# Cluster attention and two MLPs on one core: the softmax reciprocals and scalings of two units taken together

## The chip, the core and the metric

The kernel runs on one core of a Trainium2 chip. The metric is device time in microseconds (us) of one execution. The kernel before was timed three times: the median is 837.77 us, the lowest 836.97, the highest 840.25. The profile that is read below comes from another execution, which took 837.66 us.

## The reference

What is computed, in numpy: attention in which a query sees only the keys of its own cluster, followed by two MLPs. Shapes: q, k and v are (2, 8, 768, 64), there are 16 centroids a head; x is (1536, 512), the first MLP is 1536 wide inside and the second 2048.

```python
q_assign = np.argmax(np.einsum('bhsd,hcd->bhsc', q_n, c_n), axis=-1)   # q_n, k_n, c_n: rows of unit length
k_assign = np.argmax(np.einsum('bhsd,hcd->bhsc', k_n, c_n), axis=-1)
mask = q_assign[:, :, :, None] == k_assign[:, :, None, :]
scores = scale * np.matmul(q, k.transpose(0, 1, 3, 2))
scores = np.where(mask, scores, -1000000000.0)
scores = scores - np.max(scores, axis=-1, keepdims=True)
attn = np.exp(scores)
attn = attn / (np.sum(attn, axis=-1, keepdims=True) + 1e-09)
attn_out = np.matmul(attn, v)
x = attn_out.transpose(0, 2, 1, 3).reshape(B * S, H * D)
x = (1.0 / (1.0 + np.exp(-(x @ w_gate))) * (x @ w_val)) @ w_out
h = np.maximum(x @ w_in2, 0.0)
out = h * h @ w_out2
```

## The kernel before, in words

The kernel has an attention stage and then the two MLPs. The order of the instructions on each engine is the order in which the code issues them; each engine works through its own queue in that order, and semaphores hold an instruction until what it needs is there.

The attention is cut into 96 **units** of 128 queries: 8 pairs of heads (`pairs`), two heads each (`e`), two halves of the queries (`n`), three blocks of 128 in each half (`j`). The main loop (line 888) has one **step** n for each unit and a few more at the end. A unit passes through several steps:

- Its scores, 128 queries by 768 keys in four matmuls into PSUM tile `s`, are issued by TensorE in the step before its own (`scores`, line 776).
- In step n VectorE takes the negative maximum of each row (line 897), and ScalarE the exponential into tile `p`, with the row sums as a second result (line 918; the trace shows the fetch of the sums as a short instruction of its own, ACTIVATION_READ_ACCUMULATOR). GpSimd adds 1e-9 to the sums (line 932).
- In step n+1 VectorE takes the reciprocal of the sums and GpSimd scales `p` by it, in place (`normalise`, lines 847 and 848).
- In step n+3 (`LAG = 3`) the scaled unit is moved out (`evac`): TensorE transposes its six blocks into two PSUM tiles `t` (line 794), ScalarE copies them rounded into `pt_hi` (line 796), and VectorE subtracts what was kept to get `pt_lo` (line 802).
- After three units, TensorE multiplies `pt_hi` and `pt_lo` with the values in thirds, one third a step (lines 812 and 813).

The small numbers of a unit lie in tile `nm`, a column each: negative maximum, sum, sum plus 1e-9, reciprocal. There are four buffers for `p` (`LAG + 1`), three PSUM tiles for `t`, two for `s`.

Within a step the engines get their work in this order. TensorE: the transposes of the unit of three steps before, the scores of the next unit, one third of an attention product, and preparation of the next pair of heads. VectorE: the maximum, what was left over of the preparation (`drain`), the reciprocal, the two subtractions of line 802, preparation. ScalarE: the two copies of line 796, the exponential. GpSimd: the scaling of the unit before, the addition of 1e-9, and then what `late`, `todo` and `decoding` hold for this step: splitting the values (lines 754 and 757), adding up and splitting a finished output for the MLP (lines 832, 841 and 843), a part of the argmax (line 661), in some steps a part of the decoding of the first MLP weights (lines 224 and 227). These go by tables of step numbers (`STEPS`, `VALUES`, `SUMS`, `EARLY_PARTS`).

After the 96 units the MLPs follow; their matmuls (lines 339 to 341 and 417) and the decoding of their weights don't touch the lines of the change.

Of the kernel before, what the change touches and what calls it, by code (L numbers as in the profile page):

```python
# [8 lines left out]
F32 = mybir.dt.float32  # L9
# [5 lines left out]
ALU = mybir.AluOpType  # L15
AX = mybir.AxisListType
# [52 lines left out]
def cluster_attention_two_mlps(  # L69
# [13 lines left out]
    nc = tc.nc  # L83
    B, H, S, D = q.shape
    NCL = centroids.shape[1]
    P = 128
# [6 lines left out]
    NH = HB * P  # L93
# [47 lines left out]
    def open_weights():  # L141
        for nm, bufs in (("wraw", 2), ("wtmp", 1), ("w", NW - EARLY)):
            pools[nm] = ctx.enter_context(tc.tile_pool(name=nm, bufs=bufs, side="right", reuse_waits="tile"))
        for _ in range(2):
            fetch()


    def early(spare):
        body, mag, top = (spare[:, t * DM : (t + 1) * DM] for t in range(3))
        raw = spare[:, 4 * DM :].rearrange("p (f t) -> p f t", t=2)  # L150
        fetch(raw)
        ring.extend(w_early)
        return [part for n in range(EARLY) for part in early_parts(n, (w_early[n], body, mag, f32(top)), raw)]
# [155 lines left out]
    with tc.manual_schedule():  # L309
# [4 lines left out]
        ones = const.tile([P, 1], F32, name="ones")  # L314
# [129 lines left out]
        with ExitStack() as ac:  # L444
# [8 lines left out]
            sm = ac.enter_context(tc.tile_pool(name="sm", bufs=6))  # L453
# [308 lines left out]
            units = [(i, e, n, j) for i in range(len(pairs)) for e in range(2) for n in range(2) for j in range(HB)]  # L762
            Pt, PThi, PTlo, xs, nms, decoding = {}, {}, {}, {}, {}, {}
            UPP, N = len(units) // len(pairs), len(units)
# [5 lines left out]
            def scores(u):  # L770
                i, e, n, j = u
                c = n * HB + j
                st = ps_s.tile([P, 2, 512], F32, name="s")
                for a in range(2):
                    for m in range(2):
                        nc.tensor.matmul(  # L776
                            st[:, m, :NH],
                            Q[i, e][: DEPTH[e][a], a, c * P : (c + 1) * P],
                            K[i, e][: DEPTH[e][a], a, m * NH : (m + 1) * NH],
                            start=(a == 0),  # L780
                            stop=(a == 1),
                        )
                return st

            def evac(u, a):

                i, e, n, j = u
                if a == 0 and j == 0:
                    PThi[i, e, n] = ptp.tile([P, NB, NH], F32R, name="pt_hi")
                    PTlo[i, e, n] = ptp.tile([P, NB, NH], F32R, name="pt_lo")  # L790
                tp = ps_t.tile([P, HB, P], F32, name="t")
                for m in range(HB):
                    c = a * HB + m
                    nc.tensor.transpose(tp[:, m, :], Pt[u][:, c * P : (c + 1) * P], ident)  # L794
                hi = PThi[i, e, n][:, a * HB : (a + 1) * HB, j * P : (j + 1) * P]
                nc.scalar.copy(hi, tp)  # L796
                return tp, hi

            def low(u, a, tp, hi):
                i, e, n, j = u  # L800
                lo = PTlo[i, e, n][:, a * HB : (a + 1) * HB, j * P : (j + 1) * P]
                nc.vector.tensor_tensor(out=lo, in0=tp, in1=f32(hi), op=ALU.subtract)  # L802
# [40 lines left out]
                        nc.gpsimd.tensor_tensor(out=lo, in0=src, in1=f32(hi), op=ALU.subtract)  # L843
                    c0 = c1

            def normalise(p, nm):
                nc.vector.reciprocal(out=nm[:, 3:4], in_=nm[:, 2:3])  # L847
                nc.gpsimd.tensor_scalar(out=p, in0=p, scalar1=nm[:, 3:4], scalar2=ones, op0=ALU.mult, op1=ALU.mult)  # L848

            load(0, "kq")  # L850
            load(1, "kq")
# [11 lines left out]
            def drain():  # L863
                while posts:
                    posts.pop(0)()

            def do(f, *args):
                post = f(*args)
                if post is not None:
                    posts.append(post)  # L870
# [7 lines left out]
            outs, late, st = {}, {}, {}  # L878
# [9 lines left out]
            for n in range(N + LAG + 4):  # L888
                u = units[n] if n < N else None
                w = units[n - LAG] if 0 <= n - LAG < N else None  # L890
                if n == N - UPP:
                    drain()
                    pc.close()
                    open_weights()
                if u is not None:
                    nms[n] = sm.tile([P, 4], F32, name="nm")
                    nc.vector.tensor_reduce(out=nms[n][:, 0:1], in_=st[n][:, :, :NH], axis=AX.XY, op=ALU.max, negate=True)  # L897
                nm = nms.pop(n - 1, None)
                if nm is not None:
                    p = Pt[units[n - 1]]  # L900
                drain()
                if nm is not None and w is None:
                    normalise(p, nm)
                if n == N:
                    sc.close()
                    for nm_, bufs in (("sg", 2), ("act", NA)):
                        pools[nm_] = ctx.enter_context(tc.tile_pool(name=nm_, bufs=bufs, side="right", reuse_waits="tile"))
                    pools["a"] = ctx.enter_context(
                        tc.tile_pool(name="ps_a", bufs=4, space=PSUM, side="right", reuse_waits="tile")
                    )  # L910
                if w is not None:
                    t0, h0 = evac(w, 0)
                    t1, h1 = evac(w, 1)
                if n + 1 < N:
                    st[n + 1] = scores(units[n + 1])
                if u is not None:
                    e = pp.tile([P, S], F32, name="p")
                    nc.scalar.activation(  # L918
                        out=e.rearrange("p (m n) -> p m n", m=2),
                        in_=st.pop(n)[:, :, :NH],  # L920
                        func=AF.Exp,
                        bias=nms[n][:, 0:1],
                        accum_out=nms[n][:, 1:2],
                    )
                    Pt[u] = e
                if w is not None:
                    if nm is not None:
                        normalise(p, nm)
                    low(w, 0, t0, h0)
                    low(w, 1, t1, h1)  # L930
                if u is not None:
                    nc.gpsimd.tensor_scalar(out=nms[n][:, 2:3], in0=nms[n][:, 1:2], scalar1=1e-9, scalar2=None, op0=ALU.add)
                if w is not None:
                    Pt.pop(w)
                    if w[3] == HB - 1:
                        end = n == N + LAG - 1
                        for t in range(3):
                            late.setdefault(n + 1 + (0 if end else t), []).append((attend, (*w[:3], t)))
                        if w[1] == 1:
                            for t in range(3):  # L940
                                at = n + SUMS[w[2]][t] if w[0] < len(pairs) - 1 else n + (3 if end else 6)
                                late.setdefault(at, []).append((finish, (w[0], w[2], t)))
                for f, args in late.pop(n, []):
                    do(f, *args)
                for m, group in enumerate(todo.pop(n, [])):
                    if m:
                        drain()
                    for f in group:
                        do(f)
                if n == 0:  # L950
                    for t, part in enumerate(early(spare)):
                        decoding.setdefault(EARLY_PARTS[t], []).append(part)
                for part in decoding.pop(n, []):
                    part()
                if n - N in LATE_DECODES:
                    for t, part in enumerate(decode_next()):
                        if t < 6:
                            part()
                        else:
                            decoding.setdefault(n + 1, []).append(part)  # L960
                for t, at in enumerate(LATE_GATED):
                    if n == N + at:
                        (gated_first, gated_second)[t % 2](steps[t // 2])
# [46 lines left out]
```

## Time and profile before

| | us |
|---|---|
| median of three runs | 837.77 |
| the profiled execution | 837.66 |
| its span in the profile | 835.9 |
| PE (TensorE matmuls) busy in it | 810.9, 97% of the span |
| DVE (VectorE) busy | 626.1, 75% |
| ACT (ScalarE) busy | 443.8, 53% |
| POOL (GpSimd) busy | 213.6, 26% |

The shares are means over two stages that differ. The attention units are worked on from about 24 to 267 us; GpSimd has all its work there and nothing after 300 us. In the slices of this stage VectorE, ScalarE and GpSimd are all at eight or nine tenths, and in the MLPs TensorE alone is. A row of a timeline names the start, the duration, the engine, the line, the operation with its tiles and shape, and how often it was repeated; a bracket at its end says how long the engine sat idle before it and what it waited for.

### The profile page before, as it was taken

Reading aid. Unit: us, or ns where it says so; the run is one execution under the profiler, and the core shown is the slowest. Engines: PE = TensorE matmul, PEld = TensorE weight load, DVE = VectorE, ACT = ScalarE, POOL = GpSimd, SP = SyncE. Lnnn points to the kernel's source line nnn. Section 1 sums busy time; section 2 is a strip of 40 time slices with the busy share of each in tenths; the row PEclk is TensorE's granted clock in tenths of the full one; section 3 lists DMA queues with packets and bytes.
Section 4 is the critical chain, followed back from the end, with each engine's and each line's share of the span. In section 5 each row is a group of like instructions: output and inputs, shape, how many; then the busy total and the mean of one; then the engine's idle time right before and its main releaser. Section 6 shows DMA issues by size and latency. Waiting matters only on the chain.

```text
span 835.9 us, 11628 instructions
## 1 busy us (share of the span) xinstructions
PE 810.9 (97%) x4069; PEld 689.8 (83%) x4069; DVE 626.1 (75%) x1144; ACT 443.8 (53%) x887; POOL 213.6 (26%) x347
## 2 busy tenths in 40 slices
PE   6998999999999999999999999999999999999998
PEld 4887899999998788888888888887878888888886
DVE  5897999999998378656678657888675697788533
ACT  5787888889897233442333123345654633642530
POOL 3667889888885200000000000000000000000000
PEclk8899999999999999999999999999999999999999
DMA  7454653563421122122111212202221222212012
GB/s 171 92 134 114 135 136 85 127 152 77 100 80 35 45 76 87 45 70 76 58 69 51 75 51 76 76 26 76 76 69 59 74 75 76 76 55 72 26 51 100
DMA packets 63274, 67.01 MB, mean 80 GB/s; under 512 B 28624, under 2 KB 54224, under 8 KB 63216
## 3 DMA queue, kind: packets, MB, share of 16 engines
q1 hardware_dynamic: 63216, 66.27, 28.9%
q8 instruction: 32, 0.52, 0.3%
q14 instruction: 26, 0.21, 0.1%
HBM read 45.12 MB, written 3.15 MB: 58 GB/s over the span
## 4 chain that ended last, share of the span: by engine, by line
PE 77%; DVE 12%; ACT 4%; POOL 3%; issue 2%; DMA 1%; SPq 0%; ACTq 0%; DVEq 0%; POOLq 0%
PE bank_b L417 17%; PE bank_a L340 12%; PE bank_a L341 12%; PE bank_a L339 12%; PE bank_a L417 9%; PE s L776 4%; PE t L794 4%; DVE pt_lo L802 3%; DVE nm L897 2%; PE o L812 2%; PE o L813 2%; POOL p L848 2%; PE t L613 1%; PE t L550 1%; DMA oc<-oc 1%
## 5 line engine op out<-in xcount | busy, mean ns | idle before, releaser
L340 PE MATMUL bank_a<-x_lo,w 128*128 128x512 f32 x480 | 189.3, 394 | 0.5 <-POOL x_lo L843 0.5
L341 PE MATMUL bank_a<-x_hi,w 128*128 128x512 f32 x480 | 187.7, 391 | 2.1 <-DVE w L227 2.1
L339 PE MATMUL bank_a<-x_hi,w 128*128 128x512 f32 x480 | 188.0, 392 | 0.0
L341 PEld LDWEIGHTS bank_a<-x_hi,w 128*128 128x128 f32 x480 | 90.1, 188 | 22.6 <-DVE w L227 2.5
L339 PEld LDWEIGHTS bank_a<-x_hi,w 128*128 128x128 f32 x480 | 90.1, 188 | 21.0
L340 PEld LDWEIGHTS bank_a<-x_lo,w 128*128 128x128 f32 x480 | 90.1, 188 | 20.6 <-POOL x_lo L843 1.0
L383 DVE TENSOR_TENSOR slo<-act,shi 128x512 fp32r<-128x512 f32 x84 | 57.5, 688 | 59.0 <-ACT shi L382 54.5
L802 DVE TENSOR_TENSOR pt_lo<-t,pt_hi 128x384 fp32r<-128x384 f32 x192 | 96.8, 545 | 6.0 <-ACT pt_hi L796 6.0
L848 POOL TENSOR_SCALAR p<-p,nm,ones 128x768 f32<-128x768 f32 x96 | 96.2, 1002 | 18.3 <-DVE nm L847 15.8
L918 ACT ACTIVATE p<-s,nm 128x768 f32<-128x768 f32 x96 | 88.1, 918 | 18.0 <-DVE nm L847 9.1
L776 PE MATMUL s<-st_k,st_q 128*128 128x384 f32 (+1 forms) x384 | 93.2, 365 | 0.9 <-ACT st_k L694 0.9
L897 DVE TENSOR_REDUCE nm<-s 128x1 f32<-128x768 f32 x96 | 91.0, 947 | 2.6 <-PE s L776 2.5
L794 PE MATMUL t<-ident,p 128*128 128x128 f32 x576 | 81.7, 276 | 7.7 <-DVE pt_lo L802 6.0
L796 ACT CAST pt_hi<-t 128x384 fp32r<-128x384 f32 x192 | 83.4, 488 | 8.5 <-PE t L794 7.9
L417 PE MATMUL bank_b<-wo,shi 128*128 128x512 f32 x256 | 79.3, 390 | 0.5 <-DVE wo L227 0.5
L794 PEld LDWEIGHTS t<-ident,p 128*128 128x128 f32 x576 | 65.9, 140 | 16.0 <-issue 3.6
L382 ACT CAST shi<-act 128x512 fp32r<-128x512 f32 x84 | 51.2, 615 | 52.1 <-PE bank_b L417 27.1
L221 ACT CAST w<-wtop 128x512 fp32r<-128x512 f32 x38 | 23.7, 623 | 102.9 <-DVE wtop L239 102.9
L365 DVE TENSOR_TENSOR act<-bank_a,sg 128x512 f32<-128x512 f32 x36 | 24.9, 691 | 66.6 <-PE bank_a L341 62.5
L776 PEld LDWEIGHTS s<-st_k,st_q 128*128 128x128 f32 (+1 forms) x384 | 64.2, 194 | 3.2 <-ACT p L918 1.7
L812 PE MATMUL o<-pt_hi,vt 128*128 128x384 f32 x192 | 65.1, 339 | 0.4 <-ACT oc L818 0.4
L813 PE MATMUL o<-pt_lo,vt 128*128 128x384 f32 x192 | 64.7, 337 | 0.0
(132 smaller groups left out, 1381.1 us busy)
## 6 DMA issues: line engine op xcount, KB each, us to landing
wraw<-in_moe_w_out_dram SPq DMA_DIRECT2D x28, 512.0 KB, 3.2
wraw<-in_moe_w_in_dram SPq DMA_DIRECT2D x16, 512.0 KB, 3.8
wraw<-in_moe_w_gate_dram SPq DMA_DIRECT2D x11, 512.0 KB, 3.6
wraw<-in_moe_w_val_dram SPq DMA_DIRECT2D x11, 512.0 KB, 3.5
nat_v<-in_v_dram SPq DMA_DIRECT2D x8, 384.0 KB, 3.3
st_k<-st_k SPq DMA_DIRECT2D x16, 192.0 KB, 4.7
x<-oc SPq DMA_DIRECT2D x32, 96.0 KB, 2.1
out_dram<-part SPq DMA_DIRECT2D x12, 256.0 KB, 2.1
```

The costliest lines, as they stand in the source:

```text
L339: nc.tensor.matmul(bk, w[:, 0, ks], mov_hi[:, kk], start=(kk == 0), stop=False)
L340: nc.tensor.matmul(bk, w[:, 0, ks], mov_lo[:, kk], start=False, stop=False)
L341: nc.tensor.matmul(bk, w[:, 1, ks], mov_hi[:, kk], start=False, stop=(kk == KD - 1))
L417: nc.tensor.matmul(bk, st, mv, start=(first and n == 0), stop=(last and n == 2))
L776: nc.tensor.matmul(st[:, m, :NH], Q[i, e][: DEPTH[e][a], a, c * P : (c + 1) * P], K[i, e][: DEPTH[e][a], a, m * NH : (m + 1) * NH], start= ...
L794: nc.tensor.transpose(tp[:, m, :], Pt[u][:, c * P : (c + 1) * P], ident)
L796: nc.scalar.copy(hi, tp)
L802: nc.vector.tensor_tensor(out=lo, in0=tp, in1=f32(hi), op=ALU.subtract)
L812: nc.tensor.matmul(o, vt, hi[:, c, :], start=(c == 0), stop=False)
L848: nc.gpsimd.tensor_scalar(out=p, in0=p, scalar1=nm[:, 3:4], scalar2=ones, op0=ALU.mult, op1=ALU.mult)
L897: nc.vector.tensor_reduce(out=nms[n][:, 0:1], in_=st[n][:, :, :NH], axis=AX.XY, op=ALU.max, negate=True)
L918: nc.scalar.activation(out=e.rearrange("p (m n) -> p m n", m=2), in_=st.pop(n)[:, :, :NH], func=AF.Exp, bias=nms[n][:, 0:1], accum_out=nms ...
```

## The change

Two units, an even one and the odd one behind it, share one tile `nm`, now four rows of two columns. The exponential and the maximum of each unit write its own column. The addition of 1e-9 is issued once for both, in the step of the odd unit. `normalise` is issued in the next even step only: one reciprocal of both columns, and then the two scalings, one behind the other.

```diff
-            def normalise(p, nm):
-                nc.vector.reciprocal(out=nm[:, 3:4], in_=nm[:, 2:3])
-                nc.gpsimd.tensor_scalar(out=p, in0=p, scalar1=nm[:, 3:4], scalar2=ones, op0=ALU.mult, op1=ALU.mult)
+            def normalise(ps, nm):
+                nc.vector.reciprocal(out=nm[:, 3], in_=nm[:, 2])
+                for x, p in enumerate(ps):
+                    nc.gpsimd.tensor_scalar(
+                        out=p, in0=p, scalar1=nm[:, 3, x : x + 1], scalar2=ones, op0=ALU.mult, op1=ALU.mult
+                    )
...
                 if u is not None:
-                    nms[n] = sm.tile([P, 4], F32, name="nm")
-                    nc.vector.tensor_reduce(out=nms[n][:, 0:1], in_=st[n][:, :, :NH], axis=AX.XY, op=ALU.max, negate=True)
-                nm = nms.pop(n - 1, None)
+
+                    nms[n] = nms[n - 1] if n % 2 else sm.tile([P, 4, 2], F32, name="nm")
+                    nc.vector.tensor_reduce(out=nms[n][:, 0, n % 2, None], in_=st[n][:, :, :NH], axis=AX.XY, op=ALU.max, negate=True)
+                nm = nms[n - 1] if n % 2 == 0 and 0 < n <= N else None
                 if nm is not None:
-                    p = Pt[units[n - 1]]
+                    p = [Pt[units[x]] for x in (n - 2, n - 1)]
...
-                        bias=nms[n][:, 0:1],
-                        accum_out=nms[n][:, 1:2],
+                        bias=nms[n][:, 0, n % 2, None],
+                        accum_out=nms[n][:, 1, n % 2, None],
...
-                if u is not None:
-                    nc.gpsimd.tensor_scalar(out=nms[n][:, 2:3], in0=nms[n][:, 1:2], scalar1=1e-9, scalar2=None, op0=ALU.add)
+                if u is not None and n % 2:
+                    nc.gpsimd.tensor_scalar(out=nms[n][:, 2], in0=nms[n][:, 1], scalar1=1e-9, scalar2=None, op0=ALU.add)
```

The queues change on two engines. First GpSimd's, for units 84 to 87 (the numbers behind `nm` and `p` tell buffers; lines 932 and 848 of before are lines 936 and 849 now). Before: the scaling of unit 84, and so on to the scaling of unit 87.

```order
L848 TENSOR_SCALAR p_3560<-p_3560,nm_3541,ones_78 128x768
L932 TENSOR_SCALAR nm_3574<-nm_3574 128x1
L848 TENSOR_SCALAR p_3591<-p_3591,nm_3574,ones_78 128x768
L932 TENSOR_SCALAR nm_3602<-nm_3602 128x1
L757 TENSOR_TENSOR vt_3456<-nat_v_3360,vt_3456 128x6x64
L848 TENSOR_SCALAR p_3619<-p_3619,nm_3602,ones_78 128x768
L932 TENSOR_SCALAR nm_3631<-nm_3631 128x1
L848 TENSOR_SCALAR p_3654<-p_3654,nm_3631,ones_78 128x768
```

The same place of the changed kernel, again from what stands ahead of the scaling of unit 84 to the scaling of unit 87:

```order
L936 TENSOR_SCALAR nm_3414<-nm_3414 128x2
L849 TENSOR_SCALAR p_3433<-p_3433,nm_3414,ones_78 128x768
L849 TENSOR_SCALAR p_3463<-p_3463,nm_3414,ones_78 128x768
L757 TENSOR_TENSOR vt_3332<-nat_v_3242,vt_3332 128x6x64
L936 TENSOR_SCALAR nm_3472<-nm_3472 128x2
L849 TENSOR_SCALAR p_3489<-p_3489,nm_3472,ones_78 128x768
L849 TENSOR_SCALAR p_3523<-p_3523,nm_3472,ones_78 128x768
```

The scaling of an even unit has moved behind the addition that both units share, and that stands in the step of the odd unit.

VectorE's queue, for steps 86 to 88. Before, from the maximum of unit 86 to the subtractions of step 88 (the reciprocals are those of units 85, 86 and 87):

```order
L897 TENSOR_REDUCE nm_3602<-s_3586 128x1
L847 RECIPROCAL nm_3574<-nm_3574 128x1
L802 TENSOR_TENSOR pt_lo_3544<-t_3604,pt_hi_3543 128x3x128
L802 TENSOR_TENSOR pt_lo_3544<-t_3609,pt_hi_3543 128x3x128
L897 TENSOR_REDUCE nm_3631<-s_3614 128x1
L847 RECIPROCAL nm_3602<-nm_3602 128x1
L802 TENSOR_TENSOR pt_lo_3638<-t_3639,pt_hi_3637 128x3x128
L802 TENSOR_TENSOR pt_lo_3638<-t_3644,pt_hi_3637 128x3x128
L897 TENSOR_REDUCE nm_3666<-s_3649 128x1
L847 RECIPROCAL nm_3631<-nm_3631 128x1
```

And in the changed kernel, from the same maximum to the reciprocal of units 86 and 87:

```order
L901 TENSOR_REDUCE nm_3472<-s_3458 128x1
L847 RECIPROCAL nm_3414<-nm_3414 128x2
L802 TENSOR_TENSOR pt_lo_3417<-t_3474,pt_hi_3416 128x3x128
L802 TENSOR_TENSOR pt_lo_3417<-t_3479,pt_hi_3416 128x3x128
L901 TENSOR_REDUCE nm_3472<-s_3484 128x1
L802 TENSOR_TENSOR pt_lo_3507<-t_3508,pt_hi_3506 128x3x128
L802 TENSOR_TENSOR pt_lo_3507<-t_3513,pt_hi_3506 128x3x128
L901 TENSOR_REDUCE nm_3533<-s_3518 128x1
L847 RECIPROCAL nm_3472<-nm_3472 128x2
```

The odd step has lost its reciprocal. That of an even unit stands one step later than before, behind the maximum of the unit two after it; that of an odd unit stands where it stood.

## Rows read from the trace of the kernel before

**Rows 1.** Busy time of the engines by stretch; columns named in the second row.
```profile
core 0: us, PE busy (x) PEld busy (x) DVE busy (x) ACT busy (x) POOL busy (x), PEclk, DMA share, GB/s
26.00:100.00 74.00, 66.00 (x431) 58.67 (x430) 67.75 (x140) 57.60 (x134) 55.04 (x81) 0.99 0.54 125
100.00:219.00 119.00, 117.33 (x803) 111.80 (x803) 112.30 (x237) 105.08 (x246) 103.85 (x159) 1.00 0.49 114
219.00:263.00 44.00, 43.20 (x286) 40.91 (x286) 38.97 (x83) 39.24 (x91) 39.09 (x62) 1.00 0.24 61
263.00:836.00 573.00, 565.75 (x2475) 463.03 (x2474) 393.88 (x658) 226.29 (x391) 6.36 (x9) 1.00 0.20 65
```
**Rows 2.** The chain that ended last, shares by line, 26 to 100 us.
```profile
by line: DVE pt_lo L802 15.7%; DVE nm L897 13.4%; POOL p L848 9.8%; issue 7.2%; PE t L794 4.5%; DVE spare L236 4.5%; PE s L776 3.7%; DMA oc<-oc 3.1%; POOL nm L932 2.6%; PE t L613 2.3%; DVE nm L847 2.1%; DVE mx L651 1.9%; DVE st_k L556 1.7%;
```
**Rows 3.** The same chain, 219 to 263 us.
```profile
by line: PE t L794 24.2%; PE s L776 22.9%; PE o L812 13.4%; PE o L813 12.8%; issue 6.8%; POOL p L848 6.7%; ACT pt_hi L796 3.9%; DVE pt_lo L802 2.5%; ACT p L918 2.5%; POOL nm L932 1.9%; ACT oc L818 1.6%; POOL oc L832 0.8%; DVE nm L847 0.2%; 
```
**Rows 4.** The changed lines, grouped by line: count, busy us, mean ns, idle before.
```profile
L847 DVE RECIPROCAL nm<-nm 128x1 f32<-128x1 f32 x96 | 14.9, 155 | 11.1 <-POOL nm L932 10.9
...
L848 POOL TENSOR_SCALAR p<-p,nm,ones 128x768 f32<-128x768 f32 x96 | 96.2, 1002 | 18.3 <-DVE nm L847 15.8 <-PE t L794 1.0 <-PE s L776 0.7
L932 POOL TENSOR_SCALAR nm<-nm 128x1 f32<-128x1 f32 x96 | 22.6, 235 | 19.0 <-ACT p L918 12.1
```
**Rows 5.** Timeline of steps 87 to 89, from one set of transposes on.
```profile
241.54 0.81 PE L794 MATMUL t<-ident,p 128*128 128x128 f32 x6
...
242.17 0.87 ACT L796 CAST pt_hi<-t 128x384 fp32r<-128x384 f32 x2
...
242.91 0.94 ACT L918 ACTIVATE p<-s,nm 128x768 f32<-128x768 f32 x1
...
243.43 0.98 POOL L848 TENSOR_SCALAR p<-p,nm,ones 128x768 f32<-128x768 f32 x1
...
243.63 0.95 DVE L897 TENSOR_REDUCE nm<-s 128x1 f32<-128x768 f32 x1
...
244.49 0.21 POOL L932 TENSOR_SCALAR nm<-nm 128x1 f32<-128x1 f32 x1
244.73 0.16 DVE L847 RECIPROCAL nm<-nm 128x1 f32<-128x1 f32 x1 [0.15 <-POOL nm L932]
244.81 1.00 DVE L802 TENSOR_TENSOR pt_lo<-t,pt_hi 128x384 fp32r<-128x384 f32 x2
...
245.07 0.99 POOL L848 TENSOR_SCALAR p<-p,nm,ones 128x768 f32<-128x768 f32 x1 [0.37 <-DVE nm L847]
...
245.67 0.82 PE L794 MATMUL t<-ident,p 128*128 128x128 f32 x6
```
**Rows 6.** Timelines of the first and the last of the 48 even units.
```profile
27.67 0.16 DVE L847 RECIPROCAL nm<-nm 128x1 f32<-128x1 f32 x1 [0.33 <-POOL nm L932]
...
28.20 0.82 PE L794 MATMUL t<-ident,p 128*128 128x128 f32 x6
...
261.49 0.16 DVE L847 RECIPROCAL nm<-nm 128x1 f32<-128x1 f32 x1 [0.57 <-POOL nm L932]
...
262.27 0.82 PE L794 MATMUL t<-ident,p 128*128 128x128 f32 x6
```
**Rows 7.** Timeline of steps 50 and 51, where VectorE also has the argmax.
```profile
155.56 0.15 DVE L847 RECIPROCAL nm<-nm 128x1 f32<-128x1 f32 x1
...
155.90 0.86 PE L794 MATMUL t<-ident,p 128*128 128x128 f32 x6
...
157.00 0.87 ACT L796 CAST pt_hi<-t 128x384 fp32r<-128x384 f32 x2
...
158.53 1.00 DVE L802 TENSOR_TENSOR pt_lo<-t,pt_hi 128x384 fp32r<-128x384 f32 x2
```
**Rows 8.** One step of the weight decoding on VectorE, grouped by line and shape.
```profile
L236 DVE SCALAR_TENSOR_TENSOR wbody<-wraw,wbody 128x512 int32<-128x512 int32 x5 | 3.5, 707 | 0.2
...
L236 DVE SCALAR_TENSOR_TENSOR spare<-spare 128x512 int32<-128x512 int32 x2 | 3.5, 1729 | 0.0
```

## The prediction, made before the changed kernel ran

> **What bounds the kernel now.** I read the busy time by stretch first, then the chain that ended last, then the changed lines, then timelines. By stretch [rows 1] the MLPs (263 us on) are TensorE's alone: 565.75 of 573 us, GpSimd nearly silent. Nothing of the change runs there, so whatever the attention gains or loses passes on one to one. The attention has three parts. From 26 to 100 us TensorE is busy 66.00 of 74 us and VectorE 67.75: neither leads throughout, and the chain [rows 2] passes through VectorE's subtractions and maxima (15.7% and 13.4%) and GpSimd's scaling (9.8%). From 100 to 219 us TensorE has 117.33 of 119 us and VectorE 112.30: nearly balanced. From 219 to 263 us TensorE has 43.20 of 44, and its four lines make up 73.3% of the chain [rows 3], VectorE's maximum and subtractions hardly anything. So VectorE's time counts in a part of the stage only, while a delay to TensorE counts nearly everywhere.
>
> **What the change takes away.** VectorE loses 48 of 96 reciprocals of 155 ns each [rows 4]: 7.4 us of busy time. Less of it is on the engine's path: the next instruction begins 0.08 us after the reciprocal's start [rows 5], so the lower bound is 48 x 0.08 = 3.8 us, were VectorE the bound everywhere. It is not. I let a third count, some 1.5 us. GpSimd loses 48 additions of 235 ns, 11.3 us. Its addition has 2.6% of the chain from 26 to 100 us [rows 2], 1.9 us, and half of the additions go: about 1 us. The two-column reciprocal and addition have no row here. Below, each costs what one column costs (155 and 235 ns); above, what two single ones cost (310 and 470 ns), and then the savings are gone. I take the lower end, since a second column is nothing beside the 768 columns that the same GpSimd does in 1002 ns [rows 4]. Together the change gives back 2.5 us, at most 7.4.
>
> **What it moves.** An odd unit is treated as before, except that its scaling comes 0.99 us later, behind the even one's. It is transposed a whole step later than the even unit (two steps take 4.13 us, 241.54 to 245.67 [rows 5]), and so has 2.06 us more; its delay is covered. For the even unit the reciprocal is in step n+2 in place of n+1, and TensorE transposes it at the start of step n+3. So its scaling now takes the place that the odd unit's first scaling has in the trace, and I can read from before whether that is early enough: start of that place's reciprocal, plus 0.34 us until the scaling starts, plus 0.99 us for it, against the start of the even unit's transposes.
>
> In steps 87 to 89 [rows 5]: reciprocal at 244.73, scaling 245.07 to 246.06, transposes of unit 86 at 245.67. The even unit is 0.39 us late. I did the same sum for all 48 even units, of which the first and the last are shown [rows 6]: 27.67 + 1.33 against 28.20 is 0.80 late; 261.49 + 1.33 against 262.27 is 0.55 late. 39 of the 48 are late, by 21.1 us in sum: 12 of 13 before 100 us (7.4 us), 16 of 24 from there to 219 us (7.3), all 11 after it (6.4). With the places at which the odd units' scalings in fact started, some of them behind other GpSimd work, the sum is 32.6 us. That is the ceiling of the delays, and 0 the floor, if what waits has slack elsewhere.
>
> **How much of it stays.** Three readings. *The late stretch.* There is a closed loop: transposes at 241.54, copies from 242.17 on, then the exponential 242.91 to 243.85 with the fetch of its sums, then the addition; and beside it VectorE's maximum from 243.63 [rows 5]. Before, the addition had to wait for a scaling that stood ahead of it on GpSimd (243.43 to 244.41); this one moves away, so the reciprocal can go as the maximum ends, with the same overlap of 0.08 us as between the next two instructions (244.73 + 0.16 against 244.81): 243.63 + 0.95 - 0.08, at 244.50 in place of 244.73. The scaling then ends at 244.50 + 1.33 = 245.83, and TensorE starts no sooner: 4.29 us a round in place of 4.13. That is 0.16 us for a round in which GpSimd has nothing between addition and scaling; in about half of the rounds it has a job of 0.5 to 1 us there. So 11 rounds cost between 11 x 0.16 = 1.8 and the full 6.4 us; I take the middle, 4.1. *The middle stretch.* Three of its latenesses, 2.8 us of 7.3, are of the kind at 155.56 [rows 7]: 155.56 + 1.33 against 155.90, 0.99 late. But there the copies start only at 157.00 and the subtractions at 158.53, held by VectorE's argmax work and not by the transposes, so TensorE can be late for nothing. I let half of the 7.3 stay, 3.6. *The early stretch.* TensorE is idle 8.0 of 74 us [rows 1], so some delays fall into waits that are there; but GpSimd's own queue is full too, and the even unit now stands behind jobs of the odd step. Half again: 3.7. Together 11.4 us; the 2.5 us given back off: 8.9. For the GpSimd jobs that stand between addition and scaling (of 0.5 to 1 us, in half of 48 rounds, most of it hidden behind the maximum) I add 1.5. The net is +10.4 us, and the profiled execution's 837.66 us (span 835.9 and 1.76 around it) becomes 848.1. It lies 0.11 us under the median of the three runs, so nothing is to be corrected. I predict 848 us.
>
> Behind a reciprocal that waits, VectorE has the two subtractions of its step and the next maximum; behind the subtractions wait the PSUM tiles that TensorE's next transposes need. This is why I expect the loop to close and not to run free.
>
> **Rivals.**
> 1. *The delays vanish and only the savings remain.* If the delays are taken up by waits that TensorE has anyway, the result is 837.66 less 2.5, 835; with all 7.4 us of the reciprocals it is 830. It decides from the point at which less of the 21.1 us stays than 2.5. For it: the middle stretch has 8 units of 24 that are not late, and its largest latenesses lie in front of VectorE's argmax. Against it: all 11 of the late stretch, where TensorE has 0.8 us of idle time in 44. Chance 0.20: 0.14 within the bound of 0.5% (4.2 us, about what a measurement of this kernel can tell from no change), 0.06 beyond it.
> The Trainium skill (Perfetto Trace Analysis, Optimizing Scalar/DVE Operations) speaks for this rival: it gives a VectorE instruction on SBUF an overhead of about 60 ns and says that grouping helps where the engine is saturated. By it, as an estimate, 48 x 60 ns = 2.9 us would be won. The 0.08 us of rows 5 agrees with it in size; its condition holds in a part of the stage only.
> 2. *The delays add up in full.* Each late unit pushes all that follows: 837.66 + 21.1 = 859, and with the GpSimd work as it stood, 870. For it: the loop above is closed through all four engines. Against it: the three large ones in front of the argmax. Chance 0.15.
> 3. *Two scalings in a row block VectorE.* In the decoding of weights the same instruction takes 707 ns when GpSimd is silent and 1729 ns in the attention [rows 8], 1.02 us more, about one scaling. It reads two tensors from SBUF. VectorE's two compares of the argmax do so too, in each of 7 preparations; the later one falls into the even step, where GpSimd is now busy for 2 us on end. If each of the 7 waits for one scaling, that is 7 us on top of the forecast, 855; if both compares do, 14 us and 862. Against it: the argmax was beside scalings before, too. Chance 0.10.
> The Trainium skill (SBUF: State Buffer, section "SBUF: two separate sides") says that VectorE with two SBUF inputs and GpSimd hold a port pair in turn, for a whole instruction each. Rows 8 agree with it; by it the wait is bounded by the instruction under way, so two scalings in a row would cost no more than one.
>
> **How the numbers follow.** The forecast (half of the lateness stays, 842 to 856) has 0.55, the rivals 0.20, 0.15 and 0.10. Slower by over 0.5% are the forecast and rivals 2 and 3, less 0.02 for a forecast that ends just under the bound: 0.78. Within 0.5%: 0.14 + 0.02 = 0.16. Faster: 0.06. The range goes from 837, which leaves out most of rival 1's better half, to 860, which leaves out the upper ends of rivals 2 and 3.
>
> **What the changed profile would show.** VectorE's reciprocals: 48 of about 155 ns; GpSimd's additions: 48 of about 235 ns. If I am right, TensorE's transposes (line 794) of even units wait for GpSimd's scaling in most rounds, 0.1 to 0.6 us each; the copies of line 796 wait more; in the late stretch two steps take about 4.3 us where the trace of before has 4.13; VectorE and ScalarE are less busy by share. If rival 1 holds, the transposes show no such wait and two steps still take 4.13 us. If rival 3 holds, the argmax compares become about 1 us longer. I would be wrong if the even unit's scaling started well before 0.34 us behind the reciprocal, or if the reciprocal itself ran earlier in the step than before by more than the 0.23 us assumed (244.73 to 244.50).

## The result, and the profile after

The changed kernel takes 850.3 us in the median of six runs (847.8 to 851.15), the kernel before 837.62 in six. The ratio is 1.0141, with a 95% interval of 1.0125 to 1.0156: slower by 12.7 us, where +10.4 us and 848 us were forecast. The profiled execution took 850.01 us, with a span of 848.2.

Where the time went is seen from the transposes (line 794) of four units: the first, unit 26, unit 74 and the last. The busy time of the engines between these points, of before and then of the changed kernel (columns as in [rows 1]):

```profile
28.20:101.81 73.61, 65.61 (x430) 58.08 (x429) 68.05 (x140) 58.07 (x134) 54.17 (x79) 1.00 0.51 118
101.81:220.06 118.25, 116.58 (x799) 111.24 (x798) 111.09 (x234) 104.37 (x246) 103.83 (x159) 1.00 0.50 114
220.06:266.40 46.34, 45.54 (x296) 42.72 (x295) 41.29 (x87) 40.69 (x91) 38.90 (x62) 1.00 0.22 57
266.40:835.90 569.50, 562.35 (x2459) 460.19 (x2457) 390.97 (x653) 223.78 (x387) 5.82 (x8) 1.00 0.21 66
```
```profile
28.46:104.00 75.54, 67.33 (x428) 60.32 (x429) 66.12 (x128) 57.92 (x134) 50.78 (x66) 0.95 0.49 115
104.00:229.04 125.04, 119.15 (x798) 111.80 (x798) 111.67 (x210) 104.45 (x244) 97.00 (x135) 0.99 0.47 108
229.04:278.80 49.76, 46.35 (x294) 42.09 (x295) 40.72 (x76) 40.13 (x91) 36.97 (x52) 1.00 0.20 54
278.80:848.20 569.40, 562.30 (x2459) 460.19 (x2457) 390.95 (x653) 223.69 (x387) 5.97 (x8) 1.00 0.21 66
```

The MLPs take the same to 0.1 us. The three parts of the attention are longer by 1.9, 6.8 and 3.4 us. Every engine has the same instructions in them or fewer, and TensorE, which had 0.8 us of idle time in the third part, now has 3.4. A second thing stands in these rows: TensorE's granted clock is 0.95 in the first part and 0.99 in the second, where it was 1.00, and the same matmuls keep it busy for 67.33 and 119.15 us in place of 65.61 and 116.58. The section on two_recips comes back to it.

The chain of waits of the changed kernel, 219 to 263 us, which answers to [rows 3]:

```profile
by line: PE t L794 18.5%; POOL p L849 13.4%; PE s L776 9.6%; ACT p L922 9.1%; ACT pt_hi L796 9.0%; issue 7.0%; DVE pt_lo L802 6.5%; DVE nm L901 5.9%; PE o L812 4.0%; PE o L813 4.0%; POOL x_hi L841 3.0%; DVE oh L674 2.7%; POOL nm L936 2.0%; 
```

Before, four lines of TensorE held 73.3% of it. Now GpSimd's scaling (line 849) has doubled its share, and the exponential and the copies have larger ones too: a chain that runs round all engines.

The changed lines, grouped by line, which answer to [rows 4]:

```profile
L849 POOL TENSOR_SCALAR p<-p,nm,ones 128x768 f32<-128x768 f32 x96 | 96.5, 1013 | 21.0 <-DVE nm L847 17.0 <-PE s L776 3.9
...
L936 POOL TENSOR_SCALAR nm<-nm 128x2 f32<-128x2 f32 x48 | 11.1, 231 | 37.5 <-ACT p L922 36.8
...
L847 DVE RECIPROCAL nm<-nm 128x2 f32<-128x2 f32 x48 | 7.4, 154 | 0.6 <-POOL nm L936 0.6
```

A second column costs nothing (154 and 231 ns, 155 and 235 before). GpSimd now waits 36.8 us with the addition for the exponential, where it waited 12.1 [rows 4]; in the queue behind the addition stand the jobs of the odd step and the scaling of an even unit whose exponential is long done.

What TensorE's transposes waited for (total us and times), of before and of the changed kernel:

```profile
  DVE pt_lo L802: 7.9, 16
...
  POOL p L848: 2.9, 2
```
```profile
  POOL p L849: 38.4, 58
...
  DVE pt_lo L802: 0.2, 1
```

The total counts the matmuls' and the weight loads' idle time both (35 waits of weight loads and 23 of matmuls, against one of each), so neither number is a length of time on the path. What matters is that 35 of the 48 even units now wait for their scaling.

Two rounds of the late stretch of the changed kernel, from the transposes of even unit 80 to those of unit 84:

```profile
242.94 0.88 PE L794 MATMUL t<-ident,p 128*128 128x128 f32 x6 [0.21 <-POOL p L849]
...
245.37 0.21 POOL L936 TENSOR_SCALAR nm<-nm 128x2 f32<-128x2 f32 x1 [1.03 <-ACT p L922]
...
245.66 1.01 POOL L843 TENSOR_TENSOR x_lo<-oc,x_hi 128x384 fp32r<-128x384 f32 x1
...
245.84 0.16 DVE L847 RECIPROCAL nm<-nm 128x2 f32<-128x2 f32 x1
...
246.66 1.95 POOL L849 TENSOR_SCALAR p<-p,nm,ones 128x768 f32<-128x768 f32 x2
...
247.69 0.87 PE L794 MATMUL t<-ident,p 128*128 128x128 f32 x6 [0.40 <-POOL p L849]
...
248.28 0.86 ACT L796 CAST pt_hi<-t 128x384 fp32r<-128x384 f32 x2 [0.88 <-PE t L794]
...
248.79 1.02 DVE L802 TENSOR_TENSOR pt_lo<-t,pt_hi 128x384 fp32r<-128x384 f32 x2 [0.74 <-ACT pt_hi L796]
...
249.02 0.92 ACT L922 ACTIVATE p<-s,nm 128x768 f32<-128x768 f32 x1
...
249.73 0.95 DVE L901 TENSOR_REDUCE nm<-s 128x1 f32<-128x768 f32 x1
...
249.82 0.21 ACT L922 ACTIVATION_READ_ACCUMULATOR p<-s,nm 128x1 f32 x1
...
250.12 0.21 POOL L936 TENSOR_SCALAR nm<-nm 128x2 f32<-128x2 f32 x1 [1.03 <-ACT p L922]
...
250.59 0.15 DVE L847 RECIPROCAL nm<-nm 128x2 f32<-128x2 f32 x1
...
250.85 1.95 POOL L849 TENSOR_SCALAR p<-p,nm,ones 128x768 f32<-128x768 f32 x2 [0.52 <-DVE nm L847]
...
251.90 0.87 PE L794 MATMUL t<-ident,p 128*128 128x128 f32 x6
```

The row of 1.95 us is both scalings; the even one ends halfway, at 247.64 and 251.83, and TensorE starts 0.05 and 0.07 us later. The second round (4.21 us) is the closed loop of the prediction, and the rows show which of its two branches ends last. The addition is done at 250.33, but the reciprocal starts at 250.59, as VectorE's maximum ends. So the chain of this round runs through the copies, the subtractions, the maximum, the reciprocal, the scaling and the transposes; the exponential, its sums and the addition are done 0.26 us before it. In the first round (4.75 us) GpSimd does a split of line 843 between addition and scaling, and the scaling starts 0.82 us after the reciprocal in place of 0.26. There the other branch ends last: exponential, sums, addition, split, scaling.

### The profile page after: what moved, and what is told of

Its sections match the earlier page's. It is cut to its first block, busy times and chain, and to the rows that moved or that the text cites. A ratio compares the mean times of both kernels' runs of the same rounds, so it can differ in the third digit from the quotient of the medians.

```text
span 848.2 us, 11457 instructions
## 1 busy us (share of the span) xinstructions
PE 814.2 (96%) x4069; PEld 689.8 (81%) x4069; DVE 624.8 (74%) x1096; ACT 443.7 (52%) x887; POOL 201.5 (24%) x299
## 4 chain that ended last, share of the span: by engine, by line
PE 78%; DVE 8%; POOL 5%; ACT 5%; issue 2%; DMA 1%; SPq 0%; POOLq 0%; DVEq 0%; ACTq 0%
PE bank_b L417 16%; PE bank_a L340 12%; PE bank_a L341 12%; PE bank_a L339 12%; PE bank_a L417 9%; PE t L794 6%; PE s L776 5%; POOL p L849 3%; PE o L813 2%; PE o L812 2%; ACT p L922 1%; ACT pt_hi L796 1%; DVE pt_lo L802 1%; DVE nm L901 1%; PE t L613 1%
```

## Experiments

Theory 1 is that of the prediction: the even unit's scaling has come a step too late. Theory 2: the wider operations, or the wait for both units, cost by themselves. Theory 3: two scalings in a row, as a burst, hold other work up. Ratios are to the kernel before on the same chip, with 95% intervals.

**delay_only.** All reciprocals and additions as before; only the scaling is held until there are two.

```diff
                 nc.vector.reciprocal(out=nm[:, 3:4], in_=nm[:, 2:3])
-                nc.gpsimd.tensor_scalar(out=p, in0=p, scalar1=nm[:, 3:4], ...)
+                held.append((p, nm))
+                if len(held) == 2:
+                    for p, nm in held:
+                        nc.gpsimd.tensor_scalar(out=p, in0=p, scalar1=nm[:, 3:4], ...)
```


> The kernel before with all its 96 reciprocals and 96 additions where they were, but the scaling of an even unit issued one step later, directly ahead of the odd one's. Theory 1 (the later scaling of the even unit closes a loop through all engines): as slow as the changed kernel and slower by what the change saves, so 850 + 2.5 = 853 us (850 to 857). Theory 2 (the wider reciprocal and addition, or the addition that waits for both units, are what costs): as before, 838 us (836 to 840).

848.24 us, 1.0116 (1.0097 to 1.0135): theory 2 falls, the delay alone makes it slower. It is 2 us under the range of theory 1. Its trace shows that it is a lesser delay than I took it for in rounds without a GpSimd job:

```profile
245.65 0.16 DVE L849 RECIPROCAL nm<-nm 128x1 f32<-128x1 f32 x1 [0.90 <-POOL nm L940]
...
246.83 0.21 POOL L940 TENSOR_SCALAR nm<-nm 128x1 f32<-128x1 f32 x1 [0.61 <-ACT p L926]
...
247.13 1.96 POOL L853 TENSOR_SCALAR p<-p,nm,ones 128x768 f32<-128x768 f32 x2
...
247.51 0.15 DVE L849 RECIPROCAL nm<-nm 128x1 f32<-128x1 f32 x1
```

The even unit has its own reciprocal since the step before, so its scaling starts 0.09 us behind the addition and ahead of the odd unit's reciprocal. From unit 84 to unit 86 it takes 4.13 us, as before, and the changed kernel 4.32.

**odd_first.** Same operations, the odd unit scaled first.

```diff
-                for x, p in enumerate(ps):
+                for x, p in reversed(list(enumerate(ps))):
```


> The changed kernel with the two scalings in the other order, the odd unit's first. Same operations, same bursts on GpSimd. Theory 1: the even unit is later by one more scaling, 0.98 us, in nearly each of 48 rounds; what is absorbed in the heavier rounds taken off, +25 to +45 us on 850: 875 to 895. Theory 3 (two scalings in a row as a burst are what costs: other GpSimd work, or VectorE, is held by them): 850 us as the changed kernel (847 to 853), since the odd unit has a step of slack to give.

891.58 us, 1.064 (1.0622 to 1.0658): 41 us more than the changed kernel for the order of two instructions, 0.86 us for each of 48 pairs. The burst is the same, so theory 3 doesn't explain it. The same wait rows of its transposes, for the weight loads and matmuls together:

```profile
  POOL p L849: 117.0, 88
```

**savings_alone.** The even units' reciprocals and additions are left out and nothing is later; these units are scaled by another column, so they stay unnormalised.

```diff
-                nc.vector.reciprocal(out=nm[:, 3:4], in_=nm[:, 2:3])
+                if odd:
+                    nc.vector.reciprocal(out=nm[:, 3:4], in_=nm[:, 2:3])
+                s = nm[:, 3:4] if odd else nm[:, 0:1]
+                nc.gpsimd.tensor_scalar(out=p, in0=p, scalar1=s, ...)
...
-                if u is not None:
+                if u is not None and n % 2:
                     nc.gpsimd.tensor_scalar(out=nms[n][:, 2:3], ...)
```


> The kernel before without the reciprocal and the addition of the even units, which are scaled by another column (their negative maximum) in their old place; so the output of the even units is left unnormalised. 48 reciprocals and 48 additions less, nothing later. This bounds the savings of the change from above. Theory 1: 2.5 us less than before, 835 us (833 to 837). If the savings are worth all of the reciprocals' time: 830 us. If GpSimd's load were the bound: 826 us.

835.69 us, 0.9978 (0.9968 to 0.9989): 1.8 us by the ratio, 2.5 by the medians. Even without any delay the change had no more to win.

**after_no_add.** The addition of 1e-9 is left out for all units.

```diff
-                nc.vector.reciprocal(out=nm[:, 3], in_=nm[:, 2])
+                nc.vector.reciprocal(out=nm[:, 3], in_=nm[:, 1])
...
-                if u is not None and n % 2:
-                    nc.gpsimd.tensor_scalar(out=nms[n][:, 2], in0=nms[n][:, 1], scalar1=1e-9, ...)
```

> The changed kernel without the addition of 1e-9 (left out for all units): the reciprocal reads the sums directly. Theory 1: the addition (0.21 us) and one hand-over between engines (about 0.2 us) go out of the loop in those rounds in which the reciprocal waits for the addition rather than for the maximum; about 40 rounds show GpSimd's addition waiting for the exponential, so -4 to -12 us: 838 to 846. Theory 3 (bursts on GpSimd): the addition is small beside the two scalings, 848 to 850 us.

845.77 us, 1.0094 (1.0079 to 1.011). This gives 4.5 us back against the changed kernel (3.9 by the ratios), the small end of what theory 1 said, but not because the loop is shorter. The rounds that answer to the two above:

```profile
239.08 0.88 PE L794 MATMUL t<-ident,p 128*128 128x128 f32 x6 [0.21 <-POOL p L849]
...
240.41 0.92 ACT L922 ACTIVATE p<-s,nm 128x768 f32<-128x768 f32 x1
...
240.55 1.03 POOL L843 TENSOR_TENSOR x_lo<-oc,x_hi 128x384 fp32r<-128x384 f32 x1
...
243.35 0.87 PE L794 MATMUL t<-ident,p 128*128 128x128 f32 x6
...
247.56 0.87 PE L794 MATMUL t<-ident,p 128*128 128x128 f32 x6
```

The round without a job takes 4.21 us, as in the changed kernel: the addition was not what its reciprocal waited for. The round with the split falls from 4.75 to 4.27 us, because GpSimd, with no addition to wait with, does the split while ScalarE is still at the exponential.

**before_no_add.** The same edit on the kernel before.

> The kernel before without the addition of 1e-9 (left out for all 96 units): the reciprocal reads the sums directly; 22.6 us of GpSimd's time gone. Theory 1: the addition is rarely last in the kernel before (2.6% of the chain between 26 and 100 us), so -1 to -4 us: 834 to 837. If GpSimd's load were the bound of the attention: 826 us or less. This kernel is also a candidate that beats both.

840.01 us, 1.0028 (1.0015 to 1.0042). A miss with the wrong sign: less work, slower. It is taken up in the last section.

**after_lag4 and before_lag4.**

```diff
-            LAG = 3
+            LAG = 4
-            pp = ac.enter_context(tc.tile_pool(name="pp", bufs=LAG + 1))
+            pp = ac.enter_context(tc.tile_pool(name="pp", bufs=LAG))
```


> The changed kernel with a lag of 4 steps in place of 3 between a unit's exponential and its transposes (the pool of p keeps its four buffers). The even unit gets back the step that the change took. Theory 1: the delay is gone and the savings show, less up to 2 us for one more step at the end: 835 to 840 us. Theory 2 or 3 (wider operations, bursts): it stays at 848 to 852 us.

> The kernel before with a lag of 4 steps, as a control for the changed kernel with this lag. Theory 1: no unit is late in the kernel before, so nothing is won: 837 to 841 us (up to 2 us for one more step at the end), and the changed kernel with lag 4 lies 1 to 4 us under this one. If instead before already loses time to late scalings: 830 to 835 us.

The changed kernel: 839.18 us, 1.002 (1.0009 to 1.0031). The kernel before: 842.99, 1.0059 (1.0044 to 1.0075). With a step more to spare 2.0 us are left of the changed kernel's 12.7, and it is 3.8 us faster than before with that lag. The wait rows of its transposes for the scaling:

```profile
  POOL p L849: 1.6, 3
```

That before loses 5.8 us with this lag lies outside what I expected. Its trace shows no wait of the exponentials for a buffer of `p`; what has grown is the transposes' wait for the subtractions of line 802, 14.4 us in 25 waits where it was 7.9 in 16. Why the lag does this is not shown.

**after_jobs_even and before_jobs_even.** A first way to clear the place between addition and scaling.

```diff
-EARLY_PARTS = [5, 6, 6, 7, 8, 10, 12, 13, 17, 19, 19, 21, 27, 33, 34, 37, 37, 43]
+EARLY_PARTS = [5, 6, 6, 7, 8, 10, 12, 14, 18, 19, 19, 21, 27, 33, 34, 37, 38, 44]
-VALUES = [-3, 2, 0, 6]
-SUMS = [[5, 6, 8], [6, 8, 9]]
+VALUES = [-2, 2, 0, 6]
+SUMS = [[5, 7, 9], [6, 8, 10]]
```


> The changed kernel with GpSimd's odd-step jobs (splitting of values and outputs, parts of the weight decoding) issued one step later by the tables of step numbers, so that they stand behind the pair of scalings and no longer between the addition and the pair; only the argmax part (line 661) still stands there. In the changed kernel the 34 rounds with such a job are 11.3 us longer than before, the 14 without one 0.8 us. Theory 1 with the jobs as the larger part of the price: 3 to 7 us less than the changed kernel, 843 to 847 us. If the jobs were not the price but the step alone: 849 to 852 us.

> The kernel before with the same tables of step numbers, as a control: with a scaling in every step it makes no difference on which step the jobs stand: 836 to 840 us, as before. If the tables themselves win or lose, it shows here, and what after_jobs_even gains is to be read against it.

With these tables the last split of the second half of the queries reads the tile of the next pair of heads; the work is as much. 847.37 us, 1.0109 (1.0092 to 1.0126), and 843.42, 1.0071 (1.0055 to 1.0087). The control is not what was expected: the tables slow the kernel before by 6 us. So the pair says only that the pairing costs less with them, 4 us, and not why.

**after_jobs_moved and before_jobs_moved.** Only the dear jobs moved: four parts of the decoding and the last split of the second half of the queries. The copies of line 841 (0.5 us) that go ahead of this split come into the odd step in its place.

```diff
-EARLY_PARTS = [5, 6, 6, 7, 8, 10, 12, 13, 17, 19, 19, 21, 27, 33, 34, 37, 37, 43]
+EARLY_PARTS = [5, 6, 6, 7, 8, 10, 12, 14, 18, 19, 19, 21, 27, 33, 34, 37, 38, 48]
-SUMS = [[5, 6, 8], [6, 8, 9]]
+SUMS = [[5, 6, 8], [6, 7, 8]]
```


> The changed kernel with only the dear odd-step jobs of GpSimd moved to even steps: the four parts of the weight decoding (lines 224 and 227) and the last split of the second half of the queries (line 843, two instructions); the rest as in the changed kernel. By the rounds of the changed kernel's trace the decoding parts make three rounds 1.2 to 2.3 us longer and this split seven rounds 0.3 to 0.8 us. Theory 1 with the jobs as a part of the price: 3 to 8 us less than the changed kernel, 842 to 847 us. If only the step counts: 849 to 851 us.

> The kernel before with the same two tables, as a control. In it each step has one scaling, so an odd step is no worse a place than an even one: 837 us (836 to 840). The earlier pair of tables cost the kernel before 6 us, by crowding jobs into one step; if this pair does so too, it shows here, and the price of the pairing is the difference of the two runs.

844.05 us, 1.0063 (1.0048 to 1.0077), and the control 838.81, 1.0009 (0.9999 to 1.002), the same as before. With these jobs out of the way the pairing costs 5.2 us in place of 12.7: some 7 us of the loss hang on a few GpSimd jobs that stand between the addition and the scalings. The 5.2 us still hold others, a part of the argmax (line 661) and the split of the first half.

**two_recips.** Two one-column reciprocals in the place of the wide one.

```diff
-                nc.vector.reciprocal(out=nm[:, 3], in_=nm[:, 2])
+                for x in range(2):
+                    nc.vector.reciprocal(out=nm[:, 3, x : x + 1], in_=nm[:, 2, x : x + 1])
```


> The changed kernel with two one-column reciprocals in place of the two-column one, in the same place; everything is as late as in the changed kernel, so it measures what the wider reciprocal itself saves. In the rounds that wait for the scaling the second reciprocal adds about 0.08 us to the loop only if the scaling of the even unit waits for both; by the count of 48 x 0.08 us the wider one saves up to 3.8 us: 850 to 854 us. If the saving is off the path in a kernel that waits for scalings: 850 (849 to 851).

847.14 us, 1.0119 (1.0099 to 1.0139); the interval overlaps the changed kernel's, and neither of my two numbers fits. The profiled executions have spans of 845.1 and 848.2 us, and the reciprocal is not where they differ: nearly all of the 3.1 us lie in two rounds, from unit 12 to 14 and from unit 36 to 38. The transposes and scores at the start of the second, of the changed kernel and of two_recips:

```profile
130.63 1.24 PE L794 MATMUL t<-ident,p 128*128 128x128 f32 x6 [2.06 <-POOL p L849]
131.51 1.63 PE L776 MATMUL s<-st_k,st_q 128*128 128x384 f32 x4
```
```profile
129.10 0.87 PE L794 MATMUL t<-ident,p 128*128 128x128 f32 x6 [2.06 <-POOL p L850]
129.73 0.95 PE L776 MATMUL s<-st_k,st_q 128*128 128x384 f32 x4
```

And the whole round, of one and of the other (columns as in [rows 1]):

```profile
130.63:137.25 6.62, 6.62 (x38) 6.06 (x39) 3.08 (x7) 4.18 (x8) 4.96 (x6) 0.74 0.11 25
```
```profile
129.10:134.20 5.10, 5.10 (x37) 4.73 (x38) 3.01 (x9) 4.08 (x8) 3.93 (x5) 1.00 0.15 34
```

In both, TensorE has just waited 2.06 us for a scaling that stood behind a part of the decoding. In the changed kernel its granted clock is then 0.50 from 130.99 to 134.41 us, the lower of its two levels (1.2 GHz), and the round takes 1.5 us longer; units 12 to 14 are the same case (6.59 and 5.10 us). In two_recips the clock stays at 1.00 behind the same wait, and why it fell in one and not in the other is not shown. Apart from the clock the wide reciprocal saves nothing that can be told here and costs nothing.

No kernel here that does the whole computation beats the kernel before.

## Why the prediction was right, and where its sizes were off

- **The mechanism holds.** The even unit's transposes wait for its scaling (at 35 of 48 even units, where it was one), the loop is closed (after_lag4 opens it and only 2.0 us of the loss are left, odd_first lengthens it by 0.98 us and loses 41 more), and the delay without the fused operations is enough (delay_only). The odd unit's later scaling is covered, as said: from 247.69 the odd unit's transposes follow 2.12 us later in the changed kernel, at 249.81.
- **The clean round was sized well**, and by the branch that the prediction took, VectorE's maximum. The reciprocal was forecast 2.96 us behind the transposes' start and the round at 4.29 us; in the late stretch's three rounds without a job it comes 2.90 to 2.96 us behind, and they take 4.20, 4.32 and 4.33 us. By the changed kernel's trace 14 of the 48 rounds have nothing between addition and scaling, and they are 0.8 us longer in sum, with the two rounds at the lower clock among them.
- **The term that was mis-sized is the GpSimd jobs between addition and scaling.** I added 1.5 us for them, "most of it hidden behind the maximum". The 34 rounds with such a job are 11.3 us longer in sum, and moving the dear ones took away some 7 us. Jobs of 0.5 us are hidden for the most part; splits of line 843, the part of the argmax (1.0 us each) and the decoding (1.3 us) are not.
- **A term that the prediction does not have is TensorE's granted clock.** The two rounds at 0.74, from unit 12 to 14 and from 36 to 38, cost 3.0 us of the profiled execution's 12.3 (against two_recips), and with the jobs moved the same two rounds take 5.29 and 5.28 us, so a part of the 7 us above is the clock. Over the six runs the granted clock is 0.986 to 0.994 (of the kernel before 0.992 to 0.996 in all but one of 65); the run at 0.986 took 850.81 us and the one at 0.994 took 848.58, so most of the loss is there without it.
- **"Half of the lateness stays"** came near the measured time by luck, by two errors that cancel: for the lateness itself it was too much (5.2 us are left with the jobs moved, 7.7 with the savings of 2.5 added back, against 11.4), for the jobs too little. By stretches, net of savings: early 1.9 us, middle 6.8, late 3.4. The middle, where I let 3.6 stay, has most of the job rounds. The reading of [rows 7] held: the three units late in front of the argmax, 2.8 us in sum, cost 0.9 us over their two rounds each.
- **The savings** of 2.5 us were near what savings_alone shows (1.8 to 2.5); at a lag of 4 the two kernels lie 3.8 us apart. two_recips shows none of it from the reciprocal's width in this kernel.
- **Rival 1** fails on the waits and on the time. **Rival 2** was too dear: a part of the lateness is absorbed. **Rival 3** is there, at a smaller price. VectorE's two compares of the argmax, of before and of the changed kernel:

```profile
L658 DVE TENSOR_TENSOR eq<-tot,mx 128x384 f32<-128x384 f32 x7 | 4.8, 685 | 0.0
L674 DVE TENSOR_TENSOR oh<-eq,m 128x384 bf16<-128x384 f32 x7 | 3.9, 559 | 0.2
```
```profile
L674 DVE TENSOR_TENSOR oh<-eq,m 128x384 bf16<-128x384 f32 x7 | 6.4, 908 | 0.2
...
L658 DVE TENSOR_TENSOR eq<-tot,mx 128x384 f32<-128x384 f32 x7 | 4.0, 575 | 0.0
```

The later compare, in the even step, takes 2.4 us longer over seven: four of them 1.15 to 1.18 us, three 0.56 as before. The earlier one is 0.8 us shorter in sum. This is VectorE's busy time, of which a part at most is on the path. The price was put at 7 us.

## What to carry to other kernels

Two small operations fused over two iterations make the first iteration wait for the second: before counting the instructions saved, read from the trace when the consumer of the first one starts, against the place that the fused operation takes. A late producer costs more than its own delay where other jobs stand in its queue: look at what the queue holds between the operation that it waits for and the one that is late. And read TensorE's granted clock beside the waits, in the same rounds of both kernels: here the lower clock cost 3 of 12 us, and a difference that lies in such rounds says nothing of the edit. A lag of one more iteration, where memory allows it, is the test of such a loop.

## What the runs showed that I had not expected

In before_no_add, GpSimd works without a gap for a while; it has no addition to wait with. Its timeline from 75.71 us, and VectorE's row in the same time:

```profile
75.71 0.98 POOL L848 TENSOR_SCALAR p<-p,nm,ones 128x768 f32<-128x768 f32 x1
76.66 0.99 POOL L757 TENSOR_TENSOR vt<-nat_v,vt 128x384 fp32r<-128x384 f32 x1
77.64 0.97 POOL L848 TENSOR_SCALAR p<-p,nm,ones 128x768 f32<-128x768 f32 x1
78.59 0.99 POOL L843 TENSOR_TENSOR x_lo<-oc,x_hi 128x384 fp32r<-128x384 f32 x1
```
```profile
76.08 3.79 DVE L232 TENSOR_SCALAR spare<-spare 128x512 int32<-128x512 int32 x1
```

The other execution of this instruction in that stretch takes 0.42 us, and so (in the median) do those of the MLPs. Here it takes 3.79 us and ends 0.29 us after the last of four GpSimd instructions. In the prediction I took it that such a wait is bounded by the one instruction under way, reading the Trainium skill (SBUF — State Buffer, "SBUF: two separate sides") that way; this row, read as such a wait, is one through the rest of one and three whole ones. It costs VectorE 3.4 us. TensorE then waits 2.57 us for what stands behind it on VectorE (line 556), and at 82.82 us its granted clock falls to 0.50 (columns as in [rows 1]):

```profile
82.82:86.24 3.42, 3.42 (x14) 3.32 (x13) 3.42 (x7) 1.86 (x5) 2.86 (x4) 0.50 0.54 124
```

From unit 16 to unit 20 this kernel takes 14.97 us, the kernel before 13.64. Its ten runs have a granted clock of 0.986 to 0.992. How its loss of 2.9 us divides between such waits and the clock isn't shown, and nor is what decides who goes next.
